# Attention and a gated network on one core: a fourth exponential pattern made in place by an adding DMA, with a newly searched order of work

## The chip, the core and the metric

The kernel runs on 1 core of one Trainium2 chip. The metric is the device time of one execution in microseconds; where several runs are given, the median. A core has five engines that run their own instruction lists and wait for each other by semaphores: TensorE (PE in the profile, its weight loads PEld), VectorE (DVE), ScalarE (ACT), GpSimd (POOL) and SyncE (SP, which here only issues DMAs). Sixteen DMA engines move data between DRAM and the on-chip memory SBUF. TensorE writes its results to PSUM, eight banks of 128 x 512 float32.

## The reference

```python
x = A_x                                       # 1 x 2048 x 512, bf16
g = sigmoid((x * gate_w).sum(-1, keepdims=True))
qkv = (x @ wqkv) -> q, k, v: 32 heads of 16
p = softmax(q @ k^T * 16 ** -0.5)             # 2048 x 2048 for each head
a = (p @ v, heads joined) @ wo
b = ((x @ w_gate) * (x @ w_up)) @ w_down      # 1376 wide
out = g * a + (1 - g) * b
```

Most of the work is the 32 x 2048 x 2048 exponentials of the scores, and the products with narrow operands (16 rows of a head) before and after them.

## The kernel before

**Tiles and stages.** The 2048 queries are cut into four chunks of 512, the heads into eight groups of four. A pair of a chunk and a group is a "quad of heads", 32 in all, worked off in order; the 2048 keys are cut into 16 tiles of 128. A quad with one key tile is a step, so there are 512 steps. A step takes four groups of four small matmuls for its scores (`scores`, L1620 through `pe64`), 64 rows deep, on the upper or the lower half of TensorE's rows, each into one PSUM bank. The four banks are turned into exponentials in SBUF, and `pv` multiplies these with the values into bank 7, where the sums and the softmax denominators of the quad gather over its 16 steps. At a quad's end `o_copy` (L1830) takes bank 7 to `oc` or `oraw`. The projections of x and the gated network's matmuls (`fill`) are spread between the steps. Every engine's list is fixed before the launch.

**Two kinds of step.** In kind A, ScalarE takes the exponential of one or two neighbouring banks (`exp`, L1718): a "single" is 128 x 512, a "double" 128 x 1024. In kind D, VectorE makes it by arithmetic on bit patterns: a pass (`dpass`, L1754) adds a constant and writes the score as a 16-bit integer, which read as bf16 is a coarse power of two. Three more patterns v = 1, 2, 3 with 32 v added, each in a buffer of its own, are made by VectorE or GpSimd (`copy`, L1760 and L1764: full 128 x 2048, or halves), and `pv` adds all four, the last three with values scaled by powers of 2^(-1/4) (`Vs`). So a D step saves ScalarE four banks, and costs VectorE four passes, VectorE or GpSimd three copies and TensorE six more groups of four matmuls. The buffers are eight parts of `DB` and, once their weights are used, `wv` and `wk`. A step may be of kind D only for six of the 16 key tiles; which of these are is a result of the plan.

**The order of work.** `_Sched` (L137 on) is a planner that runs before the launch. It plays the five engines forward in time with a cost for each operation (a double or single exponential at L772, a pass at L882, delays to the next engine at L326, L356, L783, L887), and at every moment takes, for each engine, the first piece of work that a list of rules allows. `_Plan.emit` then writes each engine's list in that order, with a semaphore wait for each dependency. The rules have limits (`alook`, `dmax`, `gfull` and so on) that may change every 4 us of planned time; the tables in `PAR` (L2055 on) hold them as (repeat, value). On the chip each engine only follows its list: where an instruction waits, everything behind it on that engine waits too.

**What is there and not used.** The planner knows another way to make the pattern v = 3, which `'acc': 0` in `PAR` switches off: an adding DMA, issued by GpSimd. These lines are in the kernel before as well:

```python
        if e.acc and e.refs == 5:                      # y_unref
            self.accq.append((e, list(e.eops), self.now + self.par["adel"]))
...
        op = self.hw.accum(e.buf, deps + [self.last4]) # acc_pool, on GpSimd's list
        self.pool_v = self.lock_v = self.now + self.par["aiss"]
        t = self.dma_v = max(self.pool_v + self.par["alat"], self.dma_v + 2.65)
...
    def accum(self, buf, deps):                        # L1768
        src = bass.AP(c.tensor, c.offset, [[0, 128], [1, 2048]])
        return self.P.dma("pool", lambda e: e.dma_start(self.db[buf], src, accum_op=ALU.add), ...)
```

A step with `acc` set copies only v = 1 and v = 2. When all that reads its first pattern is done (both halves of `pv` for v = 0, and the copies), the DMA adds 96 to that pattern where it lies. Its source is one row of 2048 numbers in DRAM, read for each of the 128 partitions (512 KB in all). `pv` for v = 3 waits for the landing. GpSimd's issue also waits for VectorE's last wide copy (`last4`). The planner reckons 0.9 us for the issue (`aiss`) and 3.9 us to the landing (`alat`).

Of the kernel before, what the change touches and what calls it, by code (L numbers as in the profile page):

```python
# [136 lines left out]
class _Sched:  # L137
# [167 lines left out]
    def s_a(self, r):  # L305
# [20 lines left out]
        t = self.now + 0.385 + 0.056  # L326
# [6 lines left out]
    def s_d(self, r):  # L333
# [22 lines left out]
        t = self.now + 0.385 + 0.056  # L356
# [363 lines left out]
    def try_act(self):  # L720
# [26 lines left out]
        n = 0  # L747
# [24 lines left out]
        dur = 0.833e-3 * 512 * n + 0.051  # L772
# [10 lines left out]
        t = self.now + dur + 0.12 + 0.05  # L783
# [75 lines left out]
    def dve_pass(self, now):  # L859
# [9 lines left out]
        if self.dready and self.dready[0][0] <= now and (mate or not hold):  # L869
# [12 lines left out]
            dur = 0.065 + 0.533 * n  # L882
# [4 lines left out]
            t = self.now + dur + 0.083  # L887
# [661 lines left out]
class _Hw:  # L1549
# [376 lines left out]
    def prologue(self):  # L1926
# [119 lines left out]
        if self.par["acc"]:  # L2046
# [10 lines left out]
 'acc': 0,  # L2057
# [3 lines left out]
 'alook': ((13, 2), (5, 6), (8, 4), (6, 2), (9, 4), (3, 5), (21, 2), (3, 3), (3, 2), (1, 4), (5, 2), (18, 5),  # L2061
# [4 lines left out]
 'amax': ((7, 5), (35, 4), (6, 5), (81, 4), (6, 5), (45, 4)),  # L2066
 'amin': ((7, 3), (6, 2), (13, 4), (6, 2), (9, 3), (3, 2), (6, 4), (2, 2), (22, 3), (28, 4), (5, 3), (18, 4),
          (7, 3), (5, 4), (5, 2), (19, 4), (5, 3), (5, 4), (9, 3)),
 'apick': ((38, 0), (6, 1), (3, 0), (6, 1), (2, 0), (2, 1), (4, 0), (12, 1), (1, 0), (12, 1), (5, 0), (1, 1),
           (5, 0), (14, 1), (11, 0), (25, 1), (14, 0), (6, 1), (13, 0)),  # L2070
 'ares': ((5, 1), (6, 2), (3, 1), (21, 2), (3, 1), (6, 2), (7, 1), (1, 2), (8, 1), (17, 2), (15, 1), (6, 0),
          (24, 2), (9, 1), (9, 0), (22, 2), (18, 1)),
 'await': ((2, 0.05), (10, 0), (6, 0.05), (5, 0), (6, 0.2), (3, 0), (3, 0.2), (3, 0.1), (3, 0.2), (3, 0),
           (7, 0.05), (1, 0.2), (8, 0.05), (11, 0), (3, 0.2), (6, 0), (3, 0.4), (6, 0.05), (3, 0.1), (10, 0),
           (5, 0.4), (4, 0.2), (10, 0.05), (1, 0.4), (3, 0), (15, 0.05), (2, 0.2), (19, 0.05), (3, 0.4),
           (8, 0), (8, 0.2)),
 'cpmax': ((2, 10), (9, 6), (24, 8), (3, 5), (6, 8), (11, 2), (5, 3), (11, 6), (1, 5), (10, 10), (17, 14),
           (3, 2), (19, 8), (1, 14), (5, 6), (6, 14), (2, 10), (5, 5), (22, 8), (12, 3), (6, 8)),
 'dact': ((13, 2), (13, 3), (18, 2), (16, 3), (12, 2), (30, 3), (19, 2), (4, 3), (22, 2), (14, 3), (1, 2),
          (12, 3), (6, 2)),  # L2080
 'dahead': ((7, 0), (34, 1), (14, 0), (35, 1), (3, 0), (4, 1), (5, 0), (59, 1), (10, 0), (9, 1)),
 'dend': ((2, 2), (3, 3), (2, 1), (10, 0), (6, 3), (1, 4), (2, 1), (11, 4), (7, 3), (6, 2), (21, 3), (6, 4),
          (3, 0), (7, 4), (2, 2), (3, 4), (10, 0), (9, 4), (10, 2), (1, 3), (15, 1), (5, 3), (5, 2), (14, 0),
          (1, 4), (12, 3), (6, 2)),
 'dks': [2, 4, 7, 9, 12, 14],
 'dl': ((2, 3), (3, 4), (2, 6), (5, 4), (5, 6), (3, 5), (62, 6), (5, 4), (7, 6), (5, 5), (3, 6), (5, 4),
        (10, 6), (5, 5), (5, 6), (4, 5), (5, 6), (1, 5), (10, 6), (5, 4), (9, 6), (10, 5), (9, 6)),
 'dlook': ((29, 1), (3, 2), (70, 1), (9, 2), (1, 1), (15, 2), (13, 1), (2, 2), (19, 1), (5, 2), (14, 1)),
# [3 lines left out]
 'dmaq': 2.0,  # L2092
 'dmax': ((5, 2), (18, 3), (3, 2), (15, 3), (14, 2), (16, 3), (3, 2), (3, 3), (3, 2), (3, 3), (7, 2), (8, 3),
          (4, 2), (9, 3), (29, 2), (2, 3), (5, 2), (19, 3), (1, 2), (3, 1), (10, 2)),
 'dpair': ((17, 1), (6, 2), (3, 0), (15, 1), (14, 0), (13, 1), (6, 2), (9, 0), (4, 2), (7, 0), (1, 2), (2, 1),
           (5, 2), (9, 0), (10, 1), (10, 0), (6, 1), (10, 0), (18, 1), (1, 0), (14, 1)),
 'dpri': ((13, 1), (31, 0), (20, 1), (1, 0), (6, 1), (26, 0), (5, 1), (40, 0), (5, 1), (25, 0), (8, 1)),
 'dresv': ((67, 0), (7, 1), (7, 2), (99, 0)),
 'dwait': ((2, 0.4), (11, 0), (5, 0.2), (5, 0.4), (3, 0.1), (12, 0.2), (6, 0), (7, 0.2), (1, 0), (8, 0.2),
           (11, 0.4), (3, 0.2), (9, 0.4), (6, 0.2), (8, 0.1), (14, 0), (10, 0.2), (21, 0.4), (5, 0),  # L2100
           (14, 0.2), (6, 0.1), (3, 0), (1, 0.1), (9, 0)),
 'fcf': ((7, 1), (34, 0), (3, 1), (136, 0)),
 'fdebt': ((2, 0), (12, -10), (12, 25), (6, -30), (9, 0), (1, -30), (6, 0), (12, -10), (5, 25), (6, -30),
           (3, 0), (9, 25), (3, 10), (9, 0), (7, 25), (9, 0), (10, 10), (8, 25), (6, 0), (2, 10), (5, -10),
           (5, 10), (14, 25), (5, 0), (1, 10), (3, -10), (10, 10)),
 'ffn0': 2.6,
 'ffn1': 31.5,
 'flead': ((2, 160), (3, 0), (15, 80), (3, 160), (15, 80), (6, 160), (7, 20), (1, 160), (8, 20), (2, 80),
           (9, 10), (6, 80), (15, 160), (10, 10), (5, 40), (4, 160), (18, 80), (5, 20), (3, 0), (3, 20),
           (7, 160), (14, 80), (13, 40), (6, 80)),  # L2110
 'fmax': ((18, 3), (8, 2), (18, 3), (6, 2), (21, 1), (12, 2), (9, 3), (10, 1), (19, 3), (1, 2), (5, 3),
          (10, 2), (43, 3)),
 'fres': ((44, 0), (16, 2), (29, 0), (13, 2), (28, 0), (2, 2), (10, 1), (38, 0)),
 'fs2': ((13, 1), (22, 0), (3, 1), (6, 0), (20, 1), (10, 0), (6, 1), (3, 0), (6, 1), (3, 0), (9, 1), (20, 0),
         (4, 1), (10, 0), (5, 1), (22, 0), (18, 1)),
 'fstart': ((20, 2), (6, 1), (1, 2), (15, 1), (18, 2), (2, 1), (9, 2), (3, 1), (13, 2), (7, 1), (39, 2),
            (4, 1), (43, 2)),
 'fuse': 0,
 'fv': ((7, 1), (10, 0), (10, 1), (5, 0), (12, 1), (16, 0), (11, 1), (18, 0), (23, 1), (27, 0), (8, 1),
        (14, 0), (19, 1)),  # L2120
 'g0': 3,
 'gdue': 1.5,
 'gfull': ((2, 0.9), (24, 0.6), (6, 0.3), (9, 1.9), (3, 0.9), (3, 1.6), (4, 0.3), (16, 1.6), (10, 2.5),
           (15, 1.2), (10, 1.6), (15, 0.3), (14, 1.9), (4, 0.9), (5, 0.6), (7, 0.3), (14, 0.6), (1, 0.3),
           (5, 1.2), (13, 0.6)),
 'ghalf': ((7, 0.7), (1, 0.5), (17, 1.2), (1, 0.7), (15, 0.5), (3, 0.9), (3, 0.3), (5, 1.2), (1, 0.9),
           (14, 0.3), (5, 0.7), (6, 0.5), (5, 0.7), (19, 0.3), (19, 0.5), (8, 0.7), (5, 0.5), (6, 9),
           (7, 0.5), (10, 1.2), (8, 0.3), (2, 0.5), (13, 1.2)),
 'gwin': ((18, 0), (8, 1.2), (18, 0.5), (7, 1.2), (2, 0.5), (6, 1.2), (3, 0.2), (21, 1.2), (7, 0), (11, 1.2),
          (10, 0.5), (14, 1.2), (4, 0.5), (2, 1.2), (9, 0.8), (2, 0.5), (5, 1.2), (5, 0), (14, 0.5), (1, 1.2),  # L2130
          (13, 0)),
# [3 lines left out]
 'lg': [3, 4],  # L2135
 'mmarg': 0.6,
# [4 lines left out]
 'pfirst': ((22, 0), (4, 1), (12, 0), (33, 1), (3, 0), (28, 1), (5, 0), (12, 1), (2, 0), (9, 1), (32, 0),  # L2141
            (10, 1), (8, 0)),
# [13 lines left out]
 'skew': ((18, 3), (5, 2), (12, 4), (3, 2), (3, 4), (6, 2), (15, 3), (5, 2), (14, 6), (1, 2), (5, 4), (3, 3),  # L2156
          (2, 1), (10, 3), (19, 1), (8, 2), (3, 6), (4, 4), (4, 6), (7, 1), (14, 3), (6, 1), (13, 2)),
 'skewd': ((2, 4), (11, 2), (14, 3), (8, 4), (3, 1), (3, 4), (3, 2), (8, 3), (29, 2), (8, 3), (12, 2), (1, 3),
           (19, 4), (4, 3), (3, 2), (12, 1), (7, 4), (5, 3), (11, 2), (4, 4), (3, 3), (10, 4)),
# [16 lines left out]

# [47 lines left out]
```

## Time and profile before

| what | value |
|---|---|
| median of 3 runs | 710.07 us (707.67 to 713.38) |
| the profiled execution | 708.04 us |
| its span, first to last instruction | 706.3 us |
| TensorE's granted clock | 1.00 |
| instructions of the program | 47734 |
| moved by DMA | 22.97 MB, mean 33 GB/s |

The rows below are of four kinds. In the page's first part and in the sums over a stretch of time, each engine has its busy time and its number of instructions. A row of instructions (start, length, engine, line, operation, out<-in, count) may join several of one form; in square brackets stands the idle time of the engine ahead of it and what ended that. Durations on ScalarE and VectorE overlap with the next instruction's, so the engine's price of one is the distance of two starts. A row of waits gives who waited for whom: us in total, times, the longest. "issue" is a wait for nothing that the profile shows. A row of a DMA queue gives packets, MB and the share of 16 engines' span.

### The profile page before, as it was taken

To read this page: it belongs to the slowest core of one execution; us is meant where nothing else is said; L and a number is where in the kernel's file an instruction comes from. 1 tells how busy PE (TensorE), PEld (TensorE's weight loads), DVE (VectorE), ACT (ScalarE), POOL (GpSimd) and SP (SyncE) were. 2 spreads that over 40 slices of the span, in tenths; PEclk is the share of its full clock that TensorE was granted. 3 is DMA by queue.
4 is the path that set the end of the run, shared out by engine and by line. 5 is a ranking of instruction groups with operands and counts; after the bars stand their busy time and mean duration, and the time that the engine had idled before them with its cause. 6 is when DMAs were issued, how large, how long until landed. Compare 5 with 4: busy or idle time off the path is not lost.

```text
span 706.3 us, 47734 instructions
## 1 busy us (share of the span) xinstructions
PE 692.3 (98%) x22103; PEld 358.7 (51%) x22103; DVE 645.9 (91%) x1060; ACT 684.8 (97%) x820; POOL 450.7 (64%) x351
## 2 busy tenths in 40 slices
PE   8999999999999999999999999999999999999997
PEld 4564555554444545554554445555553555555553
DVE  5999999899999999999998998999999978989985
ACT  6899999999999999999999999999999999999994
POOL 3365658877464666655675747777666788487630
PEclk9999999999999999999999999999999999999999
DMA  9202341003010100001000010100001010000101
GB/s 156 69 6 57 78 107 36 6 20 94 16 35 5 35 18 23 28 11 28 13 23 23 15 33 19 36 13 13 27 7 40 12 36 24 14 23 18 29 19 33
DMA packets 33752, 22.97 MB, mean 33 GB/s; under 512 B 19500, under 2 KB 30156, under 8 KB 33552
## 3 DMA queue, kind: packets, MB, share of 16 engines
q1 hardware_dynamic: 32416, 18.86, 11.1%
q8 instruction: 173, 2.83, 1.6%
q0 software_dynamic: 176, 0.53, 0.3%
q10 hardware_dynamic: 960, 0.52, 0.3%
q14 instruction: 27, 0.22, 0.1%
HBM read 11.71 MB, written 2.36 MB: 20 GB/s over the span
## 4 chain that ended last, share of the span: by engine, by line
PE 90%; DVE 3%; ACT 3%; issue 1%; DMA 1%; ACTq 0%; DVEq 0%
PE ps L1620 90%; DVE DB L1754 2%; ACT xT L1718 1%; ACT PT L1718 1%; DVE DB L1760 1%; DMA DB<-in_A_x_dram 1%; ACT wu L1718 0%; DVE wv L1754 0%; DVE oc L1830 0%; DVE hT L1902 0%; PE ps L2017 0%; ACTq L1933 0%; DVE wu L1813 0%; ACT wd L1718 0%; ACT QM L2030 0%
## 5 line engine op out<-in xcount | busy, mean ns | idle before, releaser
L1620 PE MATMUL ps<-QM,KT 64*32 64x512 bf16 x8192 | 496.6, 379 | 4.2 <-issue 1.3
L1764 POOL TENSOR_TENSOR DB<-DB,cadd 128x512 int32<-128x512 int32 (+1 forms) x207 | 280.2, 1373 | 146.9 <-DVE DB L1760 62.0
L1718 ACT ACTIVATE PT<-ps 128x1024 bf16<-128x1024 f32 (+1 forms) x394 | 358.5, 1016 | 1.6 <-PE ps L1620 0.7
L1754 DVE TENSOR_SCALAR DB<-ps 128x512 int16<-128x512 f32 (+1 forms) x493 | 327.7, 692 | 31.8 <-PE ps L1620 28.3
L1620 PE MATMUL ps<-DB,Vs 64*17 64x512 bf16 x2856 | 261.6, 377 | 0.7
L1718 ACT ACTIVATE xT<-ps 128x1024 bf16<-128x1024 f32 (+1 forms) x270 | 258.6, 1043 | 1.9 <-PE ps L1620 1.7
L1620 PEld LDWEIGHTS ps<-QM,KT 64*32 64x32 bf16 x8192 | 152.2, 89 | 177.9 <-ACT PT L1718 46.9
L1620 PE MATMUL ps<-PT,Vp 64*17 64x512 bf16 x1444 | 204.5, 376 | 0.3 <-issue 0.2
L1620 PE MATMUL ps<-xT,Vp 64*17 64x512 bf16 x1030 | 165.3, 376 | 0.2
L1620 PE MATMUL ps<-xT,wu 64*32 64x512 bf16 x1376 | 111.9, 377 | 0.0
L1620 PE MATMUL ps<-xT,wg 64*32 64x512 bf16 x1376 | 110.5, 377 | 1.0 <-issue 0.9
L1760 DVE TENSOR_SCALAR DB<-DB 128x2048 int16<-128x2048 int16 (+1 forms) x160 | 107.3, 701 | 0.6 <-PE ps L1620 0.2
L1620 PE MATMUL ps<-wd,hT 64*32 64x512 bf16 x1408 | 100.2, 377 | 0.1
L1620 PE MATMUL ps<-DB,Vp 64*17 64x512 bf16 x1000 | 97.0, 377 | 0.6 <-DVE oc L1830 0.2
L1620 PEld LDWEIGHTS ps<-DB,Vs 64*17 64x17 bf16 x2856 | 70.6, 87 | 37.0 <-PE ps L1620 10.5
L1718 ACT ACTIVATE wd<-ps 128x1024 bf16<-128x1024 f32 (+1 forms) x69 | 65.7, 1059 | 0.6 <-PE ps L1620 0.4
L1764 POOL TENSOR_TENSOR DB<-wv,cadd 128x512 int32<-128x512 int32 (+1 forms) x38 | 49.7, 1331 | 24.2 <-DVE wv L1754 9.6
L1620 PEld LDWEIGHTS ps<-PT,Vp 64*17 64x17 bf16 x1444 | 51.2, 87 | 17.9 <-PE ps L1620 4.6
L1764 POOL TENSOR_TENSOR wv<-DB,cadd 128x512 int32<-128x512 int32 (+1 forms) x31 | 42.1, 1371 | 19.7 <-DVE DB L1760 7.8
L1754 DVE TENSOR_SCALAR wv<-ps 128x512 int16<-128x512 f32 x72 | 47.6, 683 | 2.5 <-PE ps L1620 2.1
L1764 POOL TENSOR_TENSOR wk<-DB,cadd 128x512 int32<-128x512 int32 (+1 forms) x30 | 39.4, 1324 | 15.8 <-DVE DB L1760 11.2
L1620 PEld LDWEIGHTS ps<-xT,Vp 64*17 64x17 bf16 x1030 | 40.8, 87 | 11.6 <-PE ps L1620 2.6
(108 smaller groups left out, 839.5 us busy)
## 6 DMA issues: line engine op xcount, KB each, us to landing
rb<-rscr SPq DMA_DIRECT2D x16, 256.0 KB
QM<-qraw SPq DMA_DIRECT2D x124, 16.0 KB, 2.3
oc<-oraw SPq DMA_DIRECT2D x60, 32.0 KB, 2.2
out_dram<-ost SPq DMA_DIRECT2D x12, 128.0 KB, 1.7
wd<-in_B_w_down_dram SPq DMA_DIRECT2D x10, 128.0 KB, 2.5
wu<-in_B_w_up_dram SPq DMA_DIRECT2D x12, 96.0 KB, 2.2
wg<-in_B_w_gate_dram SPq DMA_DIRECT2D x12, 96.0 KB, 2.6
wv<-in_A_wqkv_dram POOLq DMA_DIRECT2D x1, 512.0 KB, 5.2
```

The lines of the kernel that those rows point to most:

```text
L1620: o = pe.matmul(dst, lhs, rhs, start=st, stop=sp, tile_position=(64 * r, 32 * cc), skip_group_check=True)
L1718: return self.P.op("act", lambda a: a.activation(dst, src, ACT.Exp, scale=self.ES), deps)
L1754: return self.dve(lambda v: v.tensor_scalar(dst, src, self.YB, 0.0, ALU.add, ALU.max), deps)
L1760: return self.dve(lambda e: e.tensor_scalar(o, a, 32.0 * v, None, ALU.add), deps)
L1764: lambda e: e.tensor_tensor(o.bitcast(I32), a.bitcast(I32), self.cadd[:, v, :].bitcast(I32).to_broadcast([128, n]), ALU.add),
```

## The change

Three things in the text of the kernel:

- In the planner, an exponential costs 4 ns more (0.055 in place of 0.051, L772) and a pass 4 ns more (0.069 in place of 0.065, L882), and the delays after them 4 ns less (L783, L887), so that their results come at the same planned time and the engine is free later. Two new terms, `mga` and `mgd` (L326, L356), are zero.
- `'acc'` is a table with values of 1 to 4: so many of the first D steps of a quad make their pattern v = 3 by the adding DMA. With it the start of the kernel also fills the row in DRAM: a small memset on GpSimd and two DMAs on SP.
- Nearly all tables of limits in `PAR` have other values.

```diff
-        t = self.now + 0.385 + 0.056
+        t = self.now + 0.385 + 0.056 + self.par["mga"]
...
-        dur = 0.833e-3 * 512 * n + 0.051
+        dur = 0.833e-3 * 512 * n + 0.055
...
-        t = self.now + dur + 0.12 + 0.05
+        t = self.now + dur + 0.116 + 0.05
...
-            dur = 0.065 + 0.533 * n
+            dur = 0.069 + 0.533 * n
...
-            t = self.now + dur + 0.083
+            t = self.now + dur + 0.079
...
- 'acc': 0,
+ 'acc': ((2, 2), (17, 3), (1, 4), (28, 3), (3, 4), (5, 3), (12, 2), (26, 3), (7, 4), (9, 2), (24, 3), (3, 2),
+         (3, 3), (3, 4), (21, 3), (5, 1), (10, 2), (1, 1)),
...
- 'dresv': ((67, 0), (7, 1), (7, 2), (99, 0)),
+ 'dresv': ((2, 0), (6, 2), (12, 0), (2, 2), (8, 0), (10, 3), (3, 0), (1, 1), (12, 0), (1, 3), (8, 1), (3, 3),
+           (9, 0), (7, 3), (8, 0), (9, 1), (3, 0), (6, 1), (24, 0), (9, 1), (37, 0)),
```

What this does to the lists of the engines, by the orders of the two kernels:

| | before | after |
|---|---|---|
| steps of kind A, D | 364, 148 | 360, 152 |
| exponentials on ScalarE: double, single | 649, 158 | 566, 308 |
| passes on VectorE: of one bank, of two | 578, 7 | 598, 5 |
| copies on VectorE: full, half | 219, 15 | 188, 13 |
| copies on GpSimd: full, half | 118, 199 | 131, 79 |
| adding DMAs issued by GpSimd | 0 | 91 |
| TensorE matmuls | 22103 | 22199 |

The order in which the pieces stand is different on every engine from the first microseconds on; what is computed by the projections and the gated network is the same in number.

More of the change, by code (lines that the diff above doesn't have):

```diff
@@ L355, in s_d @@
         self.take(r, 0.216)
-        t = self.now + 0.385 + 0.056
+        t = self.now + 0.385 + 0.056 + self.par["mgd"]
         self.cnt += 1
@@ L2071 @@
[L2071 to L2084, printed above, removed]
@@ new lines @@
+ 'amin': ((2, 3), (3, 2), (5, 4), (9, 3), (3, 2), (5, 4), (16, 2), (1, 3), (4, 2), (6, 4), (2, 2), (12, 4),
+          (3, 3), (5, 2), (1, 3), (6, 2), (2, 3), (7, 4), (22, 3), (8, 2), (12, 3), (9, 4), (26, 3),
+          (11, 4)),
+ 'apick': ((2, 0), (6, 1), (15, 0), (7, 1), (10, 0), (28, 1), (3, 0), (3, 1), (11, 0), (22, 1), (10, 0),
+           (5, 1), (6, 0), (6, 1), (20, 0), (4, 1), (17, 0), (5, 1)),
+ 'ares': ((2, 1), (6, 0), (12, 2), (2, 0), (32, 2), (2, 0), (1, 1), (5, 2), (6, 1), (3, 2), (3, 0), (14, 2),
+          (13, 0), (9, 1), (3, 2), (21, 1), (6, 2), (3, 0), (11, 1), (12, 0), (14, 2)),
@@ new lines @@
+ 'await': ((8, 0.05), (11, 0.1), (1, 0), (2, 0.05), (4, 0), (2, 0.05), (12, 0.2), (13, 0.1), (4, 0),
+           (20, 0.1), (7, 0.2), (3, 0.05), (5, 0.4), (6, 0.05), (14, 0), (2, 0.1), (5, 0.05), (3, 0),
+           (6, 0.1), (6, 0), (3, 0.1), (6, 0), (23, 0.1), (12, 0.05), (2, 0.1)),
+ 'cpmax': ((2, 10), (6, 6), (4, 14), (8, 10), (19, 4), (4, 6), (1, 4), (17, 3), (1, 14), (4, 8), (2, 14),
+           (3, 10), (3, 6), (15, 10), (1, 3), (2, 2), (9, 3), (3, 2), (2, 6), (1, 14), (12, 8), (9, 14),
+           (6, 2), (8, 10), (1, 6), (3, 3), (8, 6), (2, 3), (3, 6), (10, 10), (7, 6), (4, 2)),
@@ new lines @@
+ 'dact': ((2, 2), (6, 3), (38, 2), (22, 3), (17, 2), (1, 3), (4, 2), (14, 3), (15, 2), (3, 3), (6, 2),
+          (15, 3), (23, 2), (1, 3), (10, 1), (3, 3)),
+ 'dahead': ((2, 0), (39, 1), (13, 0), (41, 1), (6, 0), (33, 1), (8, 0), (24, 1), (6, 0), (8, 1)),
+ 'dend': ((7, 2), (5, 1), (14, 4), (13, 2), (5, 5), (4, 1), (5, 4), (5, 3), (4, 0), (6, 3), (9, 4), (7, 3),
+          (2, 0), (3, 1), (5, 0), (7, 1), (9, 3), (4, 4), (5, 2), (9, 4), (6, 3), (9, 0), (6, 4), (10, 3),
+          (10, 4), (9, 5), (2, 0)),
@@ new lines @@
+ 'fmax': ((19, 3), (8, 2), (10, 3), (9, 2), (15, 1), (1, 3), (6, 2), (3, 3), (5, 2), (8, 3), (8, 2), (9, 1),
+          (11, 3), (2, 2), (5, 3), (3, 1), (6, 2), (6, 3), (9, 1), (21, 2), (8, 3), (8, 2)),
+ 'fres': ((44, 0), (13, 2), (11, 1), (20, 0), (17, 2), (5, 1), (9, 0), (3, 2), (6, 0), (6, 2), (3, 1),
+          (41, 0), (2, 2)),
+ 'fs2': ((8, 1), (9, 0), (1, 1), (2, 0), (22, 1), (35, 0), (16, 1), (21, 0), (5, 1), (21, 0), (3, 1), (25, 0),
+         (12, 1)),
+ 'fstart': ((8, 2), (5, 1), (25, 2), (20, 1), (9, 2), (1, 1), (3, 2), (5, 1), (1, 2), (7, 1), (8, 2), (18, 1),
+            (9, 2), (3, 1), (6, 2), (6, 1), (21, 2), (25, 1)),
@@ L2135 @@
  'lg': [3, 4],
+ 'mga': 0.0,
+ 'mgd': 0.0,
  'mmarg': 0.6,
```

89 lines of the change are left out of this document (40 added, 49 removed), and 27 rows, old and new, of the table PAR.

## The prediction

> **What bounds the kernel now.** I read the page's first part, then the sums by stage, cut at the first and the last copy of `oc` out of PSUM (50.6 and 678.2 us), then the rows of ScalarE.
>
> ```profile
> span 706.3 us, 47734 instructions
> ...
> PE 692.3 (98%) x22103; PEld 358.7 (51%) x22103; DVE 645.9 (91%) x1060; ACT 684.8 (97%) x820; POOL 450.7 (64%) x351
> ...
> 0.00:50.60 50.60, 46.93 (x1375) 27.01 (x1375) 41.08 (x84) 41.84 (x77) 20.62 (x23) 1.00 0.45 80
> 50.60:678.20 627.60, 622.22 (x20005) 320.34 (x20001) 586.32 (x944) 623.88 (x722) 423.74 (x324) 1.00 0.11 29
> 678.20:706.30 28.10, 23.13 (x732) 11.37 (x732) 18.53 (x34) 19.12 (x23) 6.32 (x6) 0.99 0.10 32
> ...
> 208.81 1.14 ACT L1718 ACTIVATE PT<-ps 128x1024 bf16<-128x1024 f32 x1
> ...
> 210.62 1.16 ACT L1718 ACTIVATE PT<-ps 128x1024 bf16<-128x1024 f32 x1
> ...
> 227.91 0.63 ACT L1718 ACTIVATE xT<-ps 128x512 bf16<-128x512 f32 x1
> 228.39 0.64 ACT L1718 ACTIVATE PT<-ps 128x512 bf16<-128x512 f32 x1
> ```
>
> The first three rows after the page's two are stages: length, then busy time of PE, PEld, DVE, ACT and POOL with counts, then clock, DMA share, GB/s. In the long middle ScalarE is busy 623.9 of 627.6 us. Its durations overlap: one exponential lies between the starts at 208.81 and 210.62, so a pair of banks costs 1.81 / 2 = 0.905 us of the engine, and a single one 228.39 - 227.91 = 0.48. The 649 doubles and 158 singles of the old order then take 587.3 + 75.8 = 663 us of the span of 706.3. TensorE's 98% says little, its matmuls overlap too. What it waits for says more:
>
> ```profile
> PEld ps L1620 <- ACT PT L1718: 47.4, 187, 0.8
> ...
> PEld ps L1620 <- DVE DB L1754: 31.7, 130, 0.6
> PEld ps L1620 <- PE ps L1620: 29.0, 91, 0.6
> PEld ps L1620 <- issue: 13.7, 31, 1.6
> ...
> q1 hardware_dynamic: 32416, 18.86, 11.1%
> q8 instruction: 173, 2.83, 1.6%
> q0 software_dynamic: 176, 0.53, 0.3%
> ...
> 576.76 0.09 PEld L1620 LDWEIGHTS ps<-DB,Vp 64*17 64x17 bf16 x4 [0.40 <-issue]
> ...
> 580.51 0.10 PEld L1620 LDWEIGHTS ps<-QM,KT 64*32 64x32 bf16 x4 [0.40 <-issue]
> ...
> 584.37 0.10 PEld L1620 LDWEIGHTS ps<-QM,KT 64*32 64x32 bf16 x4 [0.33 <-issue]
> ...
> 588.12 0.10 PEld L1620 LDWEIGHTS ps<-wo,OT 64*32 64x32 bf16 x4 [0.43 <-issue]
> ```
>
> Most of its idle time is for ScalarE's and VectorE's evictions. But 13.7 us are put to "issue", no engine. Four of these waits stand 3.75, 3.86 and 3.75 us apart. Queue q8 brings instructions: 173 packets for the 2 x 22103 of TensorE are 255.5 instructions, 128 matmuls, a packet. I read the even spacing as the refill of TensorE's instructions: where it is late each time, one takes (3.75 + 3.86 + 3.75) / 3 = 3.79 us. Over the span one is used up in 706.3 / 173 = 4.08 us. So the refill has 0.29 us to spare on average, and 173 x 3.79 = 656 us of refills are a second bound, about as long as ScalarE's 663.
>
> These are 2.83 MB in 173 pieces: 16.4 KB, 256 instructions. [...]
>
> Do other transfers make refills late? The bursts of `rb` (256 KB each) and the waits after them:
>
> ```profile
> 330.00:680.00 350.00, 347.38 (x11232) 179.49 (x11221) 321.83 (x515) 348.47 (x388) 243.19 (x179) 1.00 0.08 21
> ...
> 326.00:328.00 2.00, 2.00 (x80) 1.09 (x72) 2.00 (x4) 2.00 (x3) 0.41 (x1) 1.00 0.47 143
> ...
> 621.50:623.60 2.10, 2.10 (x92) 1.57 (x79) 2.10 (x4) 2.10 (x3) 1.59 (x1) 1.00 0.37 125
> 685.40:687.20 1.80, 1.80 (x80) 0.97 (x72) 1.66 (x3) 1.80 (x3) 0.00 (x0) 1.00 0.41 148
> ...
> 330.28 0.08 PEld L1620 LDWEIGHTS ps<-PT,Vp 64*17 64x17 bf16 x1 [0.48 <-issue]
> ...
> 626.30 0.09 PEld L1620 LDWEIGHTS ps<-xT,wg 64*32 64x32 bf16 x1 [0.67 <-issue]
> ...
> 688.78 0.09 PEld L1620 LDWEIGHTS ps<-PT,Vp 64*17 64x17 bf16 x2 [0.69 <-issue]
> ```
>
> Against a DMA share of 0.08 in that half of the run, three bursts with shares of 0.37 to 0.47 are each followed, 1.6 to 2.7 us after their end, by a wait for issue of 0.48 to 0.69 us, longer than the 0.33 to 0.43 of the four above. Not each of the 16 bursts does this.
>
> **The change part by part.** The order lists count, old to new:
>
> ScalarE: 649 to 566 doubles, 158 to 308 singles (of the 512 score steps, VectorE's approximate kind takes 152 instead of 148). -83 x 0.905 + 150 x 0.48 = -3.1 us, on the path that sets the end. I take -3.
>
> VectorE:
>
> ```profile
> 339.91 0.68 DVE L1754 TENSOR_SCALAR DB<-ps 128x512 int16<-128x512 f32 x1
> 340.51 0.68 DVE L1830 TENSOR_TENSOR oc<-ps,erow 128x512 f32<-128x512 f32 x1
> ...
> 335.34 1.29 DVE L1760 TENSOR_SCALAR DB<-DB 128x2048 int16<-128x2048 int16 x2
> 336.54 0.68 DVE L1754 TENSOR_SCALAR DB<-ps 128x512 int16<-128x512 f32 x1
> ...
> 301.25 4.03 POOL L1764 TENSOR_TENSOR DB<-wv,cadd 128x512 int32<-128x512 int32 x4
> ...
> L1933 POOL DMA_DIRECT2D wv<-in_A_wqkv_dram x1 | 0.8, 757 | 2.1 <-DMA wk<-in_A_wqkv_dram 2.1
> ...
> wv<-in_A_wqkv_dram POOLq DMA_DIRECT2D x1, 512.0 KB, 5.2
> ...
> 299.89 0.60 PE L1620 MATMUL ps<-QM,KT 64*32 64x512 bf16 x12
> ```
>
> A pass costs 340.51 - 339.91 = 0.60 and a wide copy (336.54 - 335.34) / 2 = 0.60. Single passes 578 to 598, double ones 7 to 5, wide copies 219 to 188, halves 15 to 13: +12.0 - 2.4 - 18.6 - 0.7 = -9.7 us. VectorE is not the bound, so most of this is idle time. Ahead of the first copy of `oc`, though, its list is shorter by five wide copies, one copy of `qraw` and three scalings, about 4 us of the 50.6. I take half, -2 (bounds 0 and -4). In the middle it shortens some of the 31.7 us that TensorE waits for passes: -2 (0 to -5).
>
> GpSimd: full copies 118 to 131, halves 199 to 79, each half 4.03 / 4 = 1.0 and each full one nearly twice that; in their place 91 DMA issues of 0.76 (the one 512 KB issue there is). 13 x 1.9 - 120 x 1.0 + 91 x 0.76 = -26 us on an engine that is idle a third of the time: nothing. The issue waits for the step's last reader, and the copies queued behind it on GpSimd wait with it; its 64% covers that.
>
> TensorE: 96 matmuls more (24 groups of four). Twelve matmuls, three groups, take 0.60, of which 0.38 is one matmul's length: 0.11 a group, +2.6 us. It has room, so I take +1. Sum of the order: -3 - 2 - 2 + 1 = -6, that is 702 against this execution's 708.0.
>
> The adds: 91 DMAs that read a 4 KB row for each of 128 partitions and add it into 512 KB. No row shows an adding DMA. Floor, the one plain 512 KB load from GpSimd: q0 holds 0.53 MB at 0.3% of 16 engines, 0.003 x 706.3 = 2.1 us of each engine. Ceiling: the destination must be read as well, twice that, 4.2. I take 2.1, the nearest row. 91 x 2.1 = 191 us, 27% of the span, against 13% for all queues of today. A refill is wanted 173 times; 47 of them would meet an add, and if the refill waits for the add's remainder on its engine, it waits evenly between 0 and 2.1 us. Beyond the 0.29 to spare that is (2.1 - 0.29)^2 / (2 x 2.1) = 0.78 us each, 37 us of TensorE. How much of it reaches the end? Rows of ScalarE beside such waits:
>
> ```profile
> 127.07 0.09 PEld L1620 LDWEIGHTS ps<-xT,wg 64*32 64x32 bf16 x1 [0.90 <-issue]
> ...
> 128.20 1.02 ACT L1718 ACTIVATE wd<-ps 128x1024 bf16<-128x1024 f32 x1 [0.38 <-PE ps L1620]
> ...
> 627.21 1.02 ACT L1718 ACTIVATE xT<-ps 128x1024 bf16<-128x1024 f32 x1 [0.35 <-PE ps L1620]
> ...
> 589.14 1.02 ACT L1718 ACTIVATE xT<-ps 128x1024 bf16<-128x1024 f32 x1 [0.53 <-PE ps L1620]
> ```
>
> The waits of 0.90, 0.67 and 0.43 idle ScalarE for 0.38, 0.35 and 0.53; after those at 576.76, 580.51 and 584.37 no row of it shows idle time. 1.26 of 3.13: I take half, since a shown idle time leaves out the overlapped tail. So +18 (bounds 0, if a refill gets its turn within an add, and 37, if all reaches the end). Sum: 708.0 - 6 + 18 = **720**. The three runs lie at 707.67 to 713.38 with a median of 710.07, the profiled one 2 us below it; I leave that in the range. About 1%, 703.0 and 717.2, is what a measurement can tell from no change.
>
> **The rivals.** Second case: the adds land late. In the new order, groups of four matmuls lie between an add's last reader and its first user: 38 at least, 52 or fewer for a quarter of the adds, 61 in the median. At 706.3 / (22103 / 4) = 0.128 us a group these are 4.9, 6.7 and 7.8 us. The plain load lands in 5.2; with a second reading 2.1 more, 7.3. Then some 40% of the 91 would be late by about 0.9 us, 33 us in TensorE's queue, where nothing passes: 702 + 33 = 735. It decides from a landing of about 6 us on.
>
> Third, the other side: a refill waits for one packet of an add, not for its rest. An add's 128 rows on 16 engines are 8 each, 2.1 / 8 = 0.26 us, below the 0.29 to spare. Then only the order counts: 702. For it: most of the 16 `rb` bursts leave no wait. Against: the three that do.
>
> Fourth: the changed order gives nothing, its gaps lie elsewhere and no refill is late: 708.
>
> [...]
>
> **How the numbers follow.** Forecast 0.46 (own range 711 to 731; a third of it below 717), late adds 0.17, third case 0.23 (half of it below 703), no gain 0.10, fifth 0.04. Slower by over 1%: 0.31 + 0.17 + 0.04 = 0.52; within: 0.15 + 0.12 + 0.10 = 0.37; faster: 0.11. The range leaves out the lower half of the third case and the upper half of the late adds: 702 to 737.
>
> **What would show it.** Right: waits of TensorE for issue near 50 us instead of 13.7, in more than 31 places, spaced by 128 matmuls, near times when q0 is busy; q0 at 27% or more of the span; ScalarE's idle time up by some 18 us, its exponentials at 660. Wrong: q0 busy and waits for issue unchanged (third case); TensorE waiting for `DMA DB<-cscr` (second); adds whose issue on GpSimd takes well over 0.8 us (fifth).

## The result, and the profile after

The changed kernel takes 808.96 us (median of 4 runs, 805.65 to 816.08) beside 710.29 for the kernel before on the same chip (707.67 to 713.38): a ratio of 1.140, 95% interval 1.131 to 1.149. The forecast was 720 with a range up to 737, so the sign is right and the size is not: the loss is 99 us where 10 were forecast. The profiled execution took 809.2 us.

From the page of the changed kernel, first the busy times, then its DMA queues (packets, MB, share of 16 engines):

```profile
span 807.4 us, 47878 instructions
...
PE 718.8 (89%) x22199; PEld 370.2 (46%) x22199; DVE 642.5 (80%) x1045; ACT 694.2 (86%) x887; POOL 439.6 (54%) x336
...
q0 software_dynamic: 13280, 48.24, 32.7%
...
q8 instruction: 173, 2.83, 1.5%
...
DB<-cscr POOLq DMA_DIRECT2D x74, 512.0 KB, 6.0
wv<-cscr POOLq DMA_DIRECT2D x11, 512.0 KB, 5.6
wk<-cscr POOLq DMA_DIRECT2D x6, 512.0 KB, 5.5
```

Every engine's share of the span has fallen, TensorE's from 98 to 89% and ScalarE's from 97 to 86%: no engine has become the bound, they wait. The 74 + 11 + 6 = 91 adds hold each DMA engine for 0.327 x 807.4 - 2.1 (the plain load of before) = 262 us, that is 2.88 us an add. They land 6.0 us after the issue. TensorE's instructions come in 173 pieces as before. The waits of the changed kernel:

```profile
PEld ps L1620 <- issue: 88.0, 98, 3.2
...
ACT PT L1718 <- PE ps L1620: 38.3, 40, 3.6
...
ACT xT L1718 <- PE ps L1620: 33.5, 32, 3.0
...
PEld ps L1620 <- DMA DB<-cscr: 21.9, 26, 2.2
...
PEld ps L1620 <- DMA wk<-cscr: 4.3, 5, 1.6
PEld ps L1620 <- DMA wv<-cscr: 4.0, 4, 1.6
```

TensorE's weight loads waited 13.7 us for issue in 31 places; now it is 88.0 in 98. New are 30.2 us of waits for patterns that the adds have not yet finished (21.9 + 4.3 + 4.0). The matmul behind a late weight load shows the same interval once more in a row of its own, so only the loads are counted. ScalarE stood idle for 21.5 us of the span before (706.3 - 684.8) and stands idle for 113.2 now (807.4 - 694.2); most of that is in the two rows of its waits for TensorE, 38.3 + 33.5 = 72 us (`PT` and `xT` both hold exponentials).

A stretch of both kinds of wait in the changed kernel, first its instructions:

```profile
86.20 1.19 POOL L1771 DMA_DIRECT2D DB<-cscr  x1
...
87.54 0.09 PEld L1620 LDWEIGHTS ps<-xT,wq 64*32 64x32 bf16 x2 [1.81 <-issue]
...
91.83 0.09 PEld L1620 LDWEIGHTS ps<-wv,Vs 64*17 64x17 bf16 x4 [1.56 <-DMA wv<-cscr]
...
95.11 0.09 PEld L1620 LDWEIGHTS ps<-DB,Vs 64*17 64x17 bf16 x2 [2.96 <-issue]
96.03 0.60 ACT L1718 ACTIVATE PT<-ps 128x512 bf16<-128x512 f32 x1 [2.39 <-PE ps L1620]
```

Then the sums of the same stretch (from:to, length, busy time and count of PE, PEld, DVE, ACT and POOL, clock, DMA share, GB/s; the share is summed over packets, and passes 1 where their recorded times overlap):

```profile
90.60:91.80 1.20, 0.17 (x7) 0.00 (x0) 0.61 (x2) 0.83 (x1) 0.04 (x1) 1.00 0.90 177
91.80:92.80 1.00, 0.81 (x17) 0.23 (x18) 0.49 (x1) 0.19 (x1) 1.00 (x1) 1.00 1.11 234
92.80:93.80 1.00, 0.00 (x0) 0.00 (x0) 0.80 (x2) 0.84 (x1) 1.00 (x2) 1.00 0.93 225
93.80:95.10 1.30, 0.00 (x0) 0.00 (x0) 0.00 (x0) 0.00 (x0) 1.22 (x2) 1.00 0.52 153
95.10:96.10 1.00, 0.99 (x39) 0.44 (x46) 0.13 (x1) 0.07 (x1) 0.00 (x0) 1.00 0.15 37
```

The two waits for issue, at 87.54 and 95.11, stand exactly 128 weight loads apart in TensorE's list, the length of one piece of instructions. In the second, TensorE runs nothing from 92.8 on. The DMA engines are full until 93.8 (shares of 0.90 to 1.11), at 0.52 until 95.1, and TensorE goes on at 95.11. VectorE and ScalarE finish what they have and stand still from 93.8. Over the whole run, 63 of the 97 distances between one of these waits and the next are a multiple of 128 weight loads, to within 4.

The trace behind the page also has the start and the length of every DMA packet, those of q8 among them, so the refills can be followed one by one. In this stretch one piece of instructions landed at 86.04 us. The next started only at 92.68, landed at 93.61, and TensorE went on 1.5 us later. Before the change, 29 of the 31 waits for issue (13.1 of 13.7 us) end 1.2 to 1.7 us after a piece has landed; in the changed kernel 71 of 98 do (78.2 of 88.0 us), where chance would give 11%. These waits are refills, and "refill waits" below are counted in this way. The other 27 waits (9.8 us) have no known cause.

A piece is not slower in its transfer: 1.01 us in the median before, 1.05 after. It starts later. Before, the next piece starts 1.05 to 1.78 us after TensorE has gone on from a refill wait. In the changed kernel it is up to 5.14 us, and later than 1.78 in 27 of 70 cases. Half a microsecond before these 27 starts, 16 packets of the adds were in flight in the median, and half a microsecond after them 1: such a piece starts where an add ends. So the mechanism of the forecast is there. What follows is about its size, and about what the forecast had not put beside it.

### The profile page after: what moved, and what is told of

Its sections match the earlier page's. It is cut to its first block, busy times and chain, and to the rows that moved or that the text cites. A ratio compares the mean times of both kernels' runs of the same rounds, so it can differ in the third digit from the quotient of the medians.

```text
span 807.4 us, 47878 instructions
## 1 busy us (share of the span) xinstructions
PE 718.8 (89%) x22199; PEld 370.2 (46%) x22199; DVE 642.5 (80%) x1045; ACT 694.2 (86%) x887; POOL 439.6 (54%) x336
## 3 DMA queue, kind: packets, MB, share of 16 engines
q0 software_dynamic: 13280, 48.24, 32.7%
## 4 chain that ended last, share of the span: by engine, by line
PE 58%; DMA 19%; issue 8%; POOL 6%; DVE 5%; ACT 2%; SPq 2%; ACTq 0%; DVEq 0%; POOLq 0%
PE ps L1620 57%; DMA DB<-cscr 9%; POOL DB L1764 4%; DMA wv<-cscr 3%; DVE DB L1754 3%; DMA wk<-cscr 2%; DMA rscr<-rec 1%; DMA rb<-rscr 1%; ACT PT L1718 1%; ACT xT L1718 1%; SPq L1840 1%; DMA QM<-qraw 1%; DMA DB<-in_A_x_dram 1%; DVE DB L1760 1%; POOL wv L1764 0%
## 5 line engine op out<-in xcount | busy, mean ns | idle before, releaser
L1620 PE MATMUL ps<-QM,KT 64*32 64x512 bf16 x8192 | 534.8, 384 | 18.6 <-issue 12.3
L1718 ACT ACTIVATE PT<-ps 128x1024 bf16<-128x1024 f32 (+1 forms) x450 | 376.8, 916 | 39.4 <-PE ps L1620 38.3
L1754 DVE TENSOR_SCALAR DB<-ps 128x512 int16<-128x512 f32 x484 | 321.4, 690 | 92.8 <-PE ps L1620 88.8
L1764 POOL TENSOR_TENSOR DB<-DB,cadd 128x1024 int32<-128x1024 int32 (+1 forms) x147 | 237.5, 1656 | 148.6 <-DVE DB L1760 44.8
L1718 ACT ACTIVATE xT<-ps 128x1024 bf16<-128x1024 f32 (+1 forms) x302 | 242.5, 872 | 34.3 <-PE ps L1620 33.5
L1620 PEld LDWEIGHTS ps<-QM,KT 64*32 64x32 bf16 x8192 | 171.3, 91 | 163.4 <-ACT PT L1718 26.9
L1620 PE MATMUL ps<-PT,Vp 64*17 64x512 bf16 x1518 | 226.1, 381 | 0.8 <-issue 0.6
L1771 POOL DMA_DIRECT2D DB<-cscr x74 | 70.0, 973 | 71.6 <-PE ps L1620 38.8
L1760 DVE TENSOR_SCALAR DB<-DB 128x2048 int16<-128x2048 int16 (+1 forms) x119 | 79.5, 699 | 1.5 <-PE ps L1620 1.2
L1923 POOL TENSOR_TENSOR OT<-oc,rb 128x512 bf16<-128x512 f32 x16 | 20.6, 1286 | 70.7 <-DMA rb<-rscr 61.5
L1764 POOL TENSOR_TENSOR DB<-wv,cadd 128x1024 int32<-128x1024 int32 (+1 forms) x21 | 36.9, 1764 | 15.6 <-DVE DB L1760 10.8
```

The costliest lines, as they stand in the source:

```text
L1620: o = pe.matmul(dst, lhs, rhs, start=st, stop=sp, tile_position=(64 * r, 32 * cc), skip_group_check=True)
L1718: return self.P.op("act", lambda a: a.activation(dst, src, ACT.Exp, scale=self.ES), deps)
L1754: return self.dve(lambda v: v.tensor_scalar(dst, src, self.YB, 0.0, ALU.add, ALU.max), deps)
L1760: return self.dve(lambda e: e.tensor_scalar(o, a, 32.0 * v, None, ALU.add), deps)
L1764: lambda e: e.tensor_tensor(o.bitcast(I32), a.bitcast(I32), self.cadd[:, v, :].bitcast(I32).to_broadcast([128, n]), ALU.add),
L1923: return self.P.op("pool", lambda g: g.tensor_tensor(self.OT[:, bi % 8, :], self.oc[:], self.rb[:], ALU.mult), deps)
```

## The experiments

**The order without the DMAs: adds made by GpSimd.** The adds of the changed kernel become operations of GpSimd on the whole pattern, in the same places.

```diff
-        return self.P.dma("pool", lambda e: e.dma_start(self.db[buf], src, accum_op=ALU.add), ...)
+        o = self.db[buf].bitcast(I32)
+        return self.P.op("pool", lambda e: e.tensor_tensor(o, o, self.cadd[:, 3, :]..., ALU.add), ...)
```

> The changed kernel's order to the last instruction, but each of the 91 adds is made by GpSimd itself, in place (one add over 128 x 1024 int32, 1.85 us by its copies), at the place in its list where the DMA was issued. Output unchanged. Three theories of the 14%. Refill (the adds keep the DMA rings busy and TensorE's instruction refills wait behind them) and landing (the adds land later than the order allows, and TensorE waits in its list) both say that all of it goes: 698 to 712 us, waits of TensorE for issue back to 10 to 20 us. Order (the new order itself does not fit the chip): above 780 us.

Measured: 748.98 us, 1.0595 [1.0565, 1.0625]. A miss. Waits for issue are gone (7.5 us), and other ones have come:

```profile
PEld ps L1620 <- DVE DB L1754: 55.8, 175, 1.6
...
PEld ps L1620 <- POOL DB L1764: 18.9, 20, 3.2
```

VectorE's busy time rose from 642.5 to 688.2 us, so this kernel exchanged one load for another and says nothing clean about the order. What GpSimd does to VectorE is taken up below.

**DMAs beside the old order.** The order of before, with 95 transfers of 512 KB into spare DRAM, issued by GpSimd, that no engine waits for. In the first kernel 91 of them add, in the second all are plain copies.

```diff
+        self.ncopy += 1
+        if self.ncopy % 7 in (2, 5) or self.ncopy in (1, 3, 4, 6):
+            i = len(self.dums) % 4
+            acc = ALU.add if len(self.dums) >= 4 else ALU.bypass
+            self.dums.append(self.P.dma("pool", lambda e: e.dma_start(self.spare[i], src, accum_op=acc), d, ...))
```

> The old kernel and its order, and beside it 95 DMAs of 512 KB from GpSimd (4 loads, then 91 adds) from the same row into a spare tensor in DRAM that nobody reads. Nothing waits for them but GpSimd's own fourth next one. Refill: an add alone takes 8 x 0.33 = 2.6 us of every ring, 37% of the refills meet one and wait for its end, TensorE's waits for issue rise by 50 to 75 us and the time to 750 to 785 us. Landing and order: nobody waits for them, 708 to 718 us.

> As the run before, but all 95 are plain copies of the same 512 KB, which take half as long in the rings (0.16 us for 4 KB). Refill: fewer refills meet one and they wait less, so the loss is a quarter to a third of the run before: 722 to 742 us. Landing and order: 708 to 718 us.

Measured: 822.6 us with adds, 1.160 [1.153, 1.168]; 754.2 with plain copies, 1.067 [1.062, 1.072]. The waits of the first (in an execution of 829.93 us, the longest of its four; the shortest took 814.89), then the waits and the queue of the second:

```profile
PEld ps L1623 <- issue: 124.2, 132, 3.7
```

```profile
PEld ps L1623 <- issue: 55.3, 82, 4.1
```

```profile
q0 software_dynamic: 13856, 50.34, 22.1%
```

Nobody reads what these DMAs write, the order is the old one, and yet the adds cost more than the whole change (115 us) and the copies 47. Of the waits for issue, 111.8 and 51.4 us are refill waits, against 13.1 before. So no late landing and no order is needed for a loss of this kind. By the queue's share (22.1% of a span of 755.9 us) a plain copy holds each engine for 1.74 us.

**What GpSimd's time alone does.** As a control of these two: in the same 95 places, two short GpSimd operations, no DMA.

```diff
+            for _ in range(2):
+                self.dums.append(self.P.op("pool", lambda e: e.tensor_tensor(self.tick[:], self.tick[:], self.tick[:], ALU.add), ...))
```

> The order of before, with two short GpSimd operations (256 numbers a row on a spare tile, some 0.5 us each) in the 95 places where the two runs with spare DMAs had their issues; no DMA is added. It is the control of those two. If GpSimd's time for the issue is what cost there, this run is near 754, the time with plain copies aside. If the DMAs themselves cost, this run stays at 707 to 714.

Measured: 767.8 us, 1.082 [1.079, 1.086]. The control failed as a control, and showed something else. Groups of VectorE's wide copies, before and in this kernel (count | busy, mean ns | idle before):

```profile
L1760 DVE TENSOR_SCALAR DB<-DB 128x2048 int16<-128x2048 int16 x150 | 103.0, 717 | 0.6 <-PE ps L1620 0.2
```

```profile
L1763 DVE TENSOR_SCALAR DB<-DB 128x2048 int16<-128x2048 int16 x150 | 140.2, 964 | 0.4
```

The same copies take 964 ns in place of 717 when GpSimd has more to do. VectorE's busy time rises from 645.9 to 706.2 us, by 60, and the span by 59.5; waits for issue stay at 8.0 us. The rows show the longer copies; by what a busier GpSimd lengthens them is in no row. In the run with plain copies aside the wide copies took 770 ns and VectorE was busy 15.8 us more than before, so about a third of that run's 47 us may be GpSimd's; its waits for issue grew by 41.6.

**TensorE's list made longer.** Two kernels tried to move the bound of the refills without any DMA, by more instructions on TensorE.

> The old kernel, with one no-operation on TensorE ahead of every group of four matmuls: some 5500 instructions more on 44200, nothing else. If TensorE lives from refills that take 3.8 us for 256 instructions, 195 of them take 739 us, and the time is 735 to 760 us with far more waits for issue, evenly spaced. [...]

> The old kernel with some 5590 instructions more on TensorE: waits on semaphores that are long reached, ahead of the groups of four matmuls (the no-operations of the fourth run are not in its trace, so that run tested nothing). 49800 instructions are 195 packets. If a refill of 256 takes 3.8 us and bounds TensorE: 739 us, so 732 to 765, waits for issue above 60 us. If refills are hidden by then: 708 to 720 us.

Measured: 707.43 us with the empty instructions, 0.9998 [0.9977, 1.0019], with the number of instructions and of pieces on q8 unchanged at 47734 and 173; so nothing was tested. With waits on semaphores that were already reached (5536 instructions more in the program): 881.72, 1.249 [1.247, 1.251]. The pieces rose to 194, but the span rose by 173.5 us, 31 ns for each wait. The busy time of the weight loads rose from 359 to 698 us, while their mean length stayed at 89 ns for the largest group: the loads overlap each other less. This price hides what the refills would have cost. The refill bound was not settled by either.

**The order, with work left out.** The add is replaced by a GpSimd operation on 64 of 2048 numbers.

```diff
-        return self.P.dma("pool", lambda e: e.dma_start(self.db[buf], src, accum_op=ALU.add), ...)
+        o = self.db[buf][:, 0:64].bitcast(I32)
+        return self.P.op("pool", lambda e: e.tensor_tensor(o, o, ..., ALU.add), ...)
```

> The changed kernel's order, with each of the 91 adds replaced by a short GpSimd operation in place on the first 64 of a row's 2048 numbers; the other 1984 of the fourth pattern are left without their 96. No DMA, and GpSimd holds nothing for long (in place of 1.85 us in the first run, which slowed VectorE's wide copies: VectorE busy 688 us there, 643 to 646 in both kernels). Refill and landing: the order alone is worth what the sum said, 696 to 710 us. Order: 740 us or more.

Measured: 705.31 us beside 705.97, 0.9989 [0.9967, 1.0011]. Its page and its wait for issue:

```profile
span 702.8 us, 47875 instructions
...
PE 690.3 (98%) x22199; PEld 364.5 (52%) x22199; DVE 633.3 (90%) x1045; ACT 681.9 (97%) x887; POOL 376.8 (54%) x336
```

```profile
PEld ps L1620 <- issue: 10.4, 26, 0.7
```

The new order itself neither wins nor loses anything that can be measured. It is the base line for the next runs, all in the changed kernel's order.

**The size and the number of the adds.** First 64 numbers of a row (16 KB) in place of 2048, then 1024 (256 KB), then every other add whole and the rest as the short operation above.

```diff
-        src = bass.AP(c.tensor, c.offset, [[0, 128], [1, 2048]])
+        src = bass.AP(c.tensor, c.offset, [[0, 128], [1, 64]])        # second kernel: 1024
-        ... e.dma_start(self.db[buf], src, accum_op=ALU.add)
+        ... e.dma_start(self.db[buf][:, 0:64], src, accum_op=ALU.add) # second kernel: 0:1024
...
+        self.nacc = getattr(self, "nacc", 0) + 1                      # third kernel
+        if self.nacc % 2:
+            o = self.db[buf][:, 0:64].bitcast(I32)
+            return self.P.op("pool", lambda e: e.tensor_tensor(o, o, ..., ALU.add), ...)
```

> The changed kernel with all its 91 adding DMAs and their waits, but each moves only the first 64 numbers of a row, 16 KB in place of 512; the rest of the fourth pattern is left without its 96. GpSimd's issue and the landing stay, the time in the rings goes. Refill: waits of TensorE for issue back to 10 to 20 us, 700 to 715 us. Landing: the fixed part of a landing (issue to use) is what costs, above 750 us.

> The order of after, each add over 1024 of the 2048 numbers of a row: 256 KB in place of 512 (the other half of each pattern is left as it was, so this part of the computation is left out). With 16 KB the time was 721, with 512 KB 809. If the cost goes with the time that an add holds the DMA engines, half of it lies near here: 755 to 770, q0 at 17 to 20% of the span. If a refill is late by the add's remainder beyond a small slack, the loss grows faster than the size: 735 to 755. If it is the landing's lateness alone, with landing near 4.6 us in place of 6.0 the waits for DB<-cscr go and the rest stays: 790 or more. The waits of PEld for issue: 50 to 65 us by the first, 35 to 50 by the second, near 88 by the third.

> The order of after, every other one of the 91 adds in place, the rest replaced by the short GpSimd operation (64 numbers of a row; what these adds would have added is left out). Between 705 with none and 809 with all: proportional gives 755 to 760. If it is two adds queued behind each other that make refills late, and one alone is mostly covered, 715 to 740. If a few adds suffice to break the run's rhythm, 775 or more.

Measured: 721.11 us with 16 KB, 1.022 [1.018, 1.025]; 745.9 with 256 KB, 1.051 [1.047, 1.056]; 759.4 with every other add, 1.070 [1.066, 1.075]. The runs were taken on several chips, on which the kernel before took 706 to 710 us, so differences of a few us between runs mean nothing. The wait for issue of the run with 16 KB:

```profile
PEld ps L1620 <- issue: 25.3, 48, 2.2
```

The queue and the waits of the run with 256 KB:

```profile
q0 software_dynamic: 13280, 24.39, 20.1%
```

```profile
PEld ps L1620 <- issue: 44.7, 59, 2.4
...
PEld ps L1620 <- DMA DB<-cscr: 2.1, 5, 0.9
...
PEld ps L1620 <- DMA wv<-cscr: 1.9, 3, 1.0
```

And of the run with every other add:

```profile
PEld ps L1620 <- issue: 48.5, 74, 3.4
...
PEld ps L1620 <- DMA DB<-cscr: 17.6, 15, 3.7
```

From 16 to 256 KB the ratio to the kernel before grows by 0.030, from 256 to 512 by 0.089: faster than the size. The number of adds counts about in proportion: 45 of the 91 cost about half of what all cost. Issuing 91 small adds, with landings at 3.7 us and 128 short packets each, costs some 15 us in itself, as much as its waits for issue grew (25.3 us in place of 10.4).

**Shorter packets, and fewer rows.** All 512 KB in rows of two pieces of 2 KB; and 120 of 128 rows.

```diff
-        src = bass.AP(c.tensor, c.offset, [[0, 128], [1, 2048]])
+        src = bass.AP(c.tensor, c.offset, [[0, 128], [0, 2], [1, 1024]])
...
+        src = bass.AP(c.tensor, c.offset, [[0, 120], [1, 2048]])      # other kernel
```

> The order of after and all 512 KB of each add, but in rows of two pieces of 1024 numbers, the first half of the constant row read twice (so the second half of a pattern gets other constants: that part of the computation is changed). If it makes packets of 2 KB, twice as many: by the theory that a refill waits for the add's whole remainder on its engine, the packet's length doesn't count, 800 to 830. By the theory that a refill gets its turn after the packet under way, its wait halves: 750 to 780, with waits of PEld for issue near 45 us. If the number of packets or descriptors is what costs, it is slower than 840.

> The changed kernel, with each add over 120 of the 128 partitions; the last 8 are left without their 96. If an add of 120 rows goes over 15 rings of 8 rows, one ring stays free. If TensorE's refills all run on that one, the waits for issue fall to 10 to 20 us and the time to 705 to 725 us. If they run on one of the 15 others, or on all, the result is within 2% of the changed kernel: 795 to 820 us.

Measured: 846.98 us with packets of 2 KB, 1.195 [1.190, 1.200], and 823.94 with 120 rows, 1.164 [1.157, 1.170]; neither helps. The queue of the run with 2 KB (24928 packets in place of 13280), and its waits:

```profile
q0 software_dynamic: 24928, 48.24, 36.3%
```

```profile
PEld ps L1620 <- issue: 113.3, 154, 3.6
...
PEld ps L1620 <- DMA DB<-cscr: 42.9, 34, 3.0
```

If a refill got its turn after the packet under way, halving the packet would have shortened its wait. The waits for issue went from 88.0 to 113.3 us, and the refill waits among them stayed: 77.0 us in place of 78.2. The time lies in the range of "the number of packets costs". The engines are held 0.363 x 849.6 - 2.1 = 306 us, 3.37 an add in place of 2.88, and the adds land at 7.0 us. What grew is the waits for late patterns (55.7 us in place of 30.2) and waits for issue that are not refills (36.3 in place of 9.8), of which a third stand ahead of weight loads that read `DB` and `Vs`, the late patterns' users.

**Late patterns without full DMA engines.** The small adds, but a pattern is ready only after a second small copy, issued by SyncE when the add has landed.

```diff
+        p = self.P.dma("pool", lambda e: e.dma_start(self.db[buf][:, 0:64], src, accum_op=ALU.add), ...)
+        return self.P.dma("sp", lambda e: e.dma_start(self.db[buf][:, 64:128], src), [p], "dlat%d" % buf)
```

> The order of after with the small adds (64 numbers of a row, 16 KB), but the pattern is ready only after a second small copy of 64 other numbers that SyncE issues when the add has landed; so the pattern is ready some 6 us after GpSimd's issue, as late as with the whole adds, while the DMA engines stay nearly idle. (Most of each add is left out, and the second copy puts constants over numbers of the pattern: that part of the computation is changed.) If lateness has its own price, the second case of the forecast, the time is 721 plus the new waits of TensorE for DB<-cscr, 25 to 35 us: 745 to 757. If late patterns only take the place of other waits, or the order has room for them, 720 to 730.

Measured: 823.06 us, 1.165 [1.161, 1.168], far above both expectations. Its queue and waits:

```profile
q0 software_dynamic: 13280, 2.02, 3.4%
```

```profile
PEld ps L1620 <- DMA DB<-cscr: 64.8, 42, 4.1
PEld ps L1620 <- issue: 46.9, 102, 3.7
PEld ps L1620 <- DMA wv<-cscr: 14.8, 7, 3.3
PEld ps L1620 <- DMA wk<-cscr: 4.5, 4, 2.1
```

The two landings in a row are 3.7 + 3.2 = 6.9 us and SyncE's issue between them, so the patterns are later here than in the changed kernel (6.0), and later than was meant. The price is steep: 84.1 us of waits for patterns in place of 30.2, nearly three times as much with patterns some 1 us later. So a late pattern has a price of its own, without full DMA engines. Only 17 of the 101 distances between this run's waits for issue are multiples of 128 weight loads, and 14.4 of the 46.9 us are refill waits. The others may be waits for the second copy; that was not tried.

**The new tables without adds, all work done.**

```diff
- 'acc': ((2, 2), (17, 3), (1, 4), ...),
+ 'acc': 0,
```

> The tables of after with the number of adds per pattern list set to none, so that GpSimd and VectorE make all patterns by copies again, and the whole computation is done. If the forecast's -6 for the searched order was right in itself, 700 to 704. If the new tables give nothing without the adds they were searched with, 706 to 720; since the numbers of copies are then not those that the tables were made for, also slower. Faster than before would make it the version that beats both.

Measured: 753.97 us, 1.067 [1.065, 1.069]. ScalarE is busy 707.3 us in place of 694.2 or 684.8: the planner, with tables made for other numbers of copies, gives ScalarE more of the steps (the list has 288 matmuls fewer than the changed kernel's, 12 steps of kind D at 24 each). This is another order, so it does not price the changed one; no version beats the kernel before.

## Why the prediction was wrong, point by point

The runs in the changed kernel's order can be put on one line, against the run with the short operations (span 702.8 us, 10.4 of issue, of which 10.1 are refill waits). All numbers are us of the profiled executions; "refills" is the part of "issue" that ends 1.2 to 1.7 us behind the landing of a piece, and "late" adds the weight loads' waits for `DB`, `wv` and `wk` from `cscr`.

| run | span more | issue more | refills of it | late | issue + late |
|---|---|---|---|---|---|
| 16 KB | 14.4 | 14.9 | 13.3 | 0 | 14.9 |
| 256 KB | 38.0 | 34.3 | 32.6 | 4.0 | 38.3 |
| every other add | 57.5 | 38.1 | 33.5 | 21.8 | 59.9 |
| the changed kernel | 104.6 | 77.6 | 68.1 | 30.2 | 107.8 |
| 120 rows | 119.9 | 71.8 | 59.4 | 38.6 | 110.4 |
| packets of 2 KB | 146.8 | 102.9 | 66.9 | 55.7 | 158.6 |
| late, small | 121.5 | 36.5 | 4.3 | 84.1 | 120.6 |

The span follows the sum of the two waits in all seven, to between 0.93 and 1.09 of it: in sum, no other wait of TensorE shrank to make room for them. At 0.97 the changed kernel's loss is 66 us of refills that come late, 29 of patterns that come late and 9 of other waits for issue, whose cause stays open. Against that the steps of the forecast:

**"47 of them would meet an add ... it waits evenly between 0 and 2.1 us", 37 us of TensorE.** The mechanism was right, the size was not. The 2.1 us was the lower of two bounds, and came from a share printed as 0.3%, one digit. The runs show 1.74 for a plain copy and 2.88 for an add. With the measured share and 2.88, the forecast's own formula gives 173 x 0.327 = 57 refills that meet an add, at (2.88 - 0.29)^2 / (2 x 2.88) = 1.16 us each: 66. To that come the 13.3 us that 16 KB adds cost already, for which the formula gives nothing: 79, and 68.1 were measured. For 256 KB it gives 19 + 13 = 32 (measured 32.6), but for every other add 36 + 7 = 43 (33.5), for 120 rows, at 2.97 us an add, 69 + 13 = 82 (59.4) and for packets of 2 KB 88 + 13 = 101 (66.9). So the formula gives the order of size, and comes out too high where the loss is largest. One reason may be that the spare time grows when TensorE waits for other things as well: in the run with 2 KB a piece is used up in 849.6 / 173 = 4.91 us and not in 4.08. That was not tried. The longest refill wait, 3.2 us, is more than one whole add less the 0.29 to spare, so some refills probably wait behind two.

The forecast's third case, a refill that waits only for one packet, is refuted: with a packet of 4 KB in flight for 0.33 us in the median, a piece that waits for one would not start up to 5.14 us after TensorE has gone on, where 1.78 was the most before; and packets of half the size did not shorten the refill waits. The starts of the late pieces above, with 16 packets of adds in flight half a microsecond before and 1 after, agree with a refill that stands behind the whole rest of an add; in what order an engine serves its queues is in no row.

**"I take half", +18.** Wrong: nearly all reached the end, 0.97 of it by the table. The half was read from ScalarE's idle time beside waits of 0.3 to 0.9 us. A wait as short as that may in part be taken up by the banks that TensorE has filled ahead, and one of 2 or 3 us may empty them: at 96.03 above, ScalarE stood idle for 2.39 of 2.96 us. With ScalarE 97% busy before, there is little room to make it good later. The sample came from the wrong sizes of wait, which a doubtful reader could have seen: the forecast's own model has waits up to 1.8 us.

**"Second case: the adds land late", 735, taken as an alternative with a chance of 0.17.** The price was about right, 33 us of TensorE against 30.2 measured, in 35 waits of 0.86 us, where some 40% of 91 at 0.9 us were forecast. That is partly luck: the forecast took it from a landing of 7.3 us, and the adds land at 6.0. The step that failed is to take it as an alternative to late refills: both occur in the same run and they add up. With adds of 16, 256 and 512 KB, which land at 3.7, 4.5 and 6.0 us, the waits for late patterns are 0, 4.0 and 30.2 us. The run with small late ones has 84 us of them with the engines nearly idle.

**The order, -6.** Not seen: 0.9989 [0.9967, 1.0011] with the order alone. ScalarE's busy time fell by 2.9 us, close to the 3.1 worked out (684.8 to 681.9), but the time did not. Even this run leaves out most of GpSimd's work for v = 3, so it favours the order.

**GpSimd's side.** Its issue takes 0.868 us in the median and up to 1.736, where 0.76 was taken. The fifth case, which the chances count with 0.04, is an issue of well over 0.8 us, and would show here. No run shows the cause that it supposed; what the runs show is an issue 0.11 us longer than the 0.76. The run with 16 KB issues as many DMAs in as long (0.870 us in the median) and loses 14.4 us of span, about its growth in waits for issue, so this case has little left to explain.

With the measured terms, the forecast's sum reads 708.0 - 3.5 (the spans, 702.8 against 706.3) + 66 + 29 + 9 = 809 in place of 708.0 - 6 + 18 = 720. It meets the profiled execution's 809.2 by construction, since the 0.97 is taken from the same span; what the runs tell is how it splits. Of what the forecast named to look for, waits for issue far above 13.7 us, at distances of 128 matmuls, with q0 over 27%, were all there, at 88.0 us and 32.7%; ScalarE's idle time rose by 92 us and not by 18.

## What to carry to other kernels

In this kernel transfers off the critical path were not free, since TensorE's instructions came late behind them: beside 95 that nobody reads, the refill waits were 111.8 us with adds and 51.4 with plain copies, against 13.1. So compare the time in which a piece of instructions is used up (4.08 us here) with the time of a refill (3.79, estimated from the spacing of the waits), and where the two are close, put a price on every bulk DMA. The refill waits grew with the time that an add holds an engine (0.29, 1.61 and 2.88 us for 16, 256 and 512 KB, by the queue's share) by 13.3, 32.6 and 68.1 us. Where two costs can occur in the same run, add them; they are not rivals. And take the share of a wait that reaches the end from waits as long as the ones to come, not from the short ones that are there.

## What the runs showed of the hardware that was not expected

- An adding DMA of 512 KB into SBUF holds each of the 16 DMA engines for 2.88 us, a plain copy of 512 KB into DRAM for 1.74. In packets of 2 KB the add takes 3.37.
- A piece of 256 instructions for TensorE is in transfer for about 1.0 us, TensorE goes on 1.2 to 1.7 us after it has landed, and behind a refill wait the next piece starts 1.05 to 1.78 us after TensorE has gone on (before the change). With the adding DMAs it starts up to 5.14 us after, and its transfer is no longer.
- VectorE's wide copies in SBUF took longer when GpSimd had more to do: 717 ns before, 964 with 190 short GpSimd operations more, 695 in the run with the short operations, where GpSimd is busy for 377 us in place of 451. GpSimd, idle a third of the time, had no free time to give here: 135 us of short operations on it came with 60 us more of VectorE's busy time and 59.5 of the span.
- A wait of TensorE on a semaphore that is already reached came to 31 ns on average here, 173.5 us for 5536 of them, and the weight loads overlapped each other less.
- TensorE's granted clock was 1.00 before, 0.982 in the changed kernel and 0.964 in the run with small late adds, beside 13.7, 118.2 and 131.0 us of waits for issue and late patterns. How much of the time that is was not tried.
